# A recurrent attention with an expert layer on one core: a tabled instruction order, column sums in parts, contiguous w_out rows, u spread on chip, and the DMA crossbar from chunk 10

## The chip, the core and the metric

The kernel runs on one core of a Trainium2 chip. The metric is the device time of one execution in microseconds; before the change it is 200.19 us (median of three runs, 199.79 to 200.97). The profile of one such execution has a span of 198.7 us from the first to the last instruction, and the clock granted to TensorE was 1.000 of full speed throughout.

The engines are PE (TensorE matmul), PEld (its weight loads), DVE (VectorE), ACT (ScalarE), POOL (GpSimd) and SP (SyncE, which here only issues DMA). An engine runs its instructions in the order in which the program emits them, so the emission order is a design choice of its own.

## What is computed

An attention with a decaying state, per batch and head, whose result feeds a two-layer expert with a squared ReLU (cut from the reference):

```python
batch, n_heads, seq, head_dim = (4, 8, 768, 48)
n_tokens, d_model, d_ff = (3072, 384, 2048)

for t in range(S):                                    # per batch and head
    cur = u * k[t] (outer) v[t]
    y[t] = r[t] @ (state + cur)
    state = w[t][:, None] * state + k[t] (outer) v[t]

h = x @ w_in            # x: y, 3072 x 384;  w_in 384 x 2048
r = maximum(h, 0)
g = s * (r * r) + b
out = g @ w_out         # w_out 2048 x 384
```

Since g = s r^2 + b, the kernel computes out = s (r^2 @ w_out) + b (column sums of w_out).

## The kernel before

The sequence is cut into 6 chunks of 128 tokens; with 4 batches there are 24 chunks n, with chunk index n // 4 and batch n % 4. Two chunks make one tile T of 256 tokens for the expert layer, so there are 12 tiles. A chunk passes through these steps (cut; each is one function of the kernel):

```python
def load(n, which):     # w, r, k, v of the chunk, 192 KB each, rows of 48 floats
    nc.sync.dma_start(out=dst, in_=src[bb, :, t0 : t0 + L, :].transpose([1, 0, 2]))
def ln(n):              # ACT: log of w
    nc.scalar.activation(out=lw[:, :, 0:D], in_=cb[n]["w"], func=AF.Ln)
def cum(n):             # PE: two triangular matmuls (running sums), and column sums
    ...
def expo(n):            # ACT: E = exp of them; lam, the decay over the chunk
    ...
def mult(n):            # DVE: prd = (r, k) * E, bf16
    ...
def trans(n):           # PE: eight transposes of prd into PSUM, n < 16
    ...
def tevac(n):           # ACT: copies them to RK in SBUF
    nc.scalar.copy(out=RK, in_=c["trps"])
def dtrans(n):          # n >= 16: the same through the DMA crossbar
    nc.sync.dma_start_transpose(out=RK, in_=c["prd"]...)
def mt(n):              # PE: eight products K R^T per chunk
    ...
def mask(n):            # DVE: times the triangular mask
    ...
def ymm(n):             # PE: y = R state (4 matmuls, not for the first chunk of a batch) + M v (8)
    ...
def dmm(n): ...         # PE: k^T v (4 matmuls); supd on DVE, sscale on POOL: the new state
def yevac(n): ...       # DVE: x = y + the diagonal part (rkp, rku, yd on POOL, cd on DVE)
def xtr(n): ...         # PE: three transposes of x, evicted by ACT (n < 16); dxtr: crossbar
```

The expert layer. A "piece" is a quarter of w_in or w_out, 768 KB in fp32, loaded into a staging buffer and cast to bf16 by ACT or POOL (w_in) or DVE (w_out):

```python
def load_wout(i):
    nc.sync.dma_start(
        out=st,
        in_=moe_w_out[i * FPP * 128 : (i + 1) * FPP * 128, :].rearrange(
            "(ft p) n -> p ft n", p=128
        ),
    )

def g1(T, i):            # one group: 2 slices of 128 rows of h, 6 matmuls 128x256
    for f in range(FPQ):
        ft = i * FPQ + f
        for kt in range(KT):
            nc.tensor.matmul(
                ps[:, f, :],
                lhsT=w_in_sb[ft // FPP][:, kt, (ft % FPP) * 128 : (ft % FPP + 1) * 128],
                rhs=xT[T][:, kt, :], ...
            )
def relu(T, i): ...      # ACT: rh = max(h, 0), bf16
def square(T, i): ...    # ACT or DVE: gT = rh * rh
def g2(T, q):            # one group: 4 matmuls 128x384 of gT with w_out, 4 groups per 128 tokens
    ...
def oevac(T, tt): ...    # DVE: out = s * o + bconst
def store(T, tt): ...    # SP: 192 KB

def colsum():
    ps = psO.tile([128, d_model], FP32, name="cs_ps", tag="o")
    for ft in range(FT):
        nc.tensor.matmul(ps, lhsT=ones, rhs=w_out_sb[ft // FPP][:, ft % FPP, :], ...)
    nc.scalar.activation(out=bconst, in_=ps, func=AF.Copy, scale=b_bc)
```

All steps are entered in a plan with an assumed duration, what they depend on and the buffers they take. When the program is built, a list scheduler walks through the plan and yields the order of emission. Loads stand in one fixed chain: four chunks and u, then the four pieces of w_in, then the four of w_out, then the other chunks. Wherever the plan sees PE idle in the first 28 us, matmuls on zeros ("warm") are emitted to keep its clock up:

```python
for t, o in pl.order():
    if o["eng"] == "PE" and t < WARM:
        warm(13 if idle_from is None else int(0.8 * (t - idle_from) / 0.11))
        idle_from = t + o["occ"]
    o["fn"](*o["args"])
```

Of the kernel before, what the change touches and what calls it, by code (L numbers as in the profile page):

```python
# [18 lines left out]
U_AT = 3.5  # L19
CIE = 'APAP'  # L20
COE = 'DDDD'
VBE = 'P'
WARM = 28.0
DTK = 16
DTX = 16
# [3 lines left out]
SLACK = 0.3  # L29


class Plan:
# [9 lines left out]
    def add(self, name, eng, occ, fn, args=(), deps=(), takes=(), prio=0.0,  # L42
            lat=0.12, port=False, dma=0.0, slack=0.0):
        self.ops[name] = dict(
            name=name, eng=eng, occ=occ, fn=fn, args=args, deps=list(deps),
            takes=list(takes), prio=prio, lat=lat, port=port, dma=dma,
            slack=slack, after=None, n=len(self.ops),
        )

    def order(self):  # L50
        ops = self.ops
        end = {}
        free = {}
        port = 0.0
        dma = 0.0
        held = {tag: [] for tag in self.rings}
        queues = {}
        for o in sorted(ops.values(), key=lambda o: (o["prio"], o["n"])):
            queues.setdefault(o["eng"], []).append(o)
        out = []  # L60

        def ready(o):
            t = 0.0
            for d in o["deps"]:
                if d not in end:
                    return None
                if d == o["after"]:
                    continue
                own = ops[d]["eng"] == o["eng"] and not ops[d]["dma"]
                t = max(t, end[d] - ops[d]["lat"] if own else end[d] + o["slack"])  # L70
            for tag, _ in o["takes"]:
                h = held[tag]
                if len(h) >= self.rings[tag]:
                    for d in h[-self.rings[tag]]:
                        if d not in end:
                            return None
                        t = max(t, end[d] + o["slack"])
            return t

        while any(queues.values()):  # L80
            best = None
            for eng, q in queues.items():
                e = free.get(eng, 0.0)
                pick = None
                for o in q:
                    r = ready(o)
                    if r is None:
                        continue
                    ask = max(r, e)
                    t = max(ask, port) if o["port"] else ask  # L90
                    if pick is None or t < pick[0] - 1e-9:
                        pick = (t, ask, o)
                if pick and (best is None or pick[:2] < best[:2]):
                    best = pick
            assert best is not None, [q[0]["name"] for q in queues.values() if q]
            t, _, o = best
            queues[o["eng"]].remove(o)
            free[o["eng"]] = t + o["occ"]
            if o["port"]:
                port = t + o["occ"]  # L100
            fin = t + o["occ"] + o["lat"]
            if o["dma"]:
                dma = max(dma, t + o["occ"] + 1.0) + o["dma"]
                fin = dma + 0.9
            end[o["name"]] = fin
            for tag, last in o["takes"]:
                held[tag].append(last)
            out.append((t, o))
        self.end = end
        self.last = out  # L110
        return out
# [3 lines left out]
def kernel(  # L115
# [60 lines left out]
    u_bc = const.tile([128, HD], FP32, name="u_bc", tag="u_bc")  # L176
    s_bc = const.tile([128, 1], FP32, name="s_bc", tag="s_bc")
# [31 lines left out]
    def coords(n):  # L209
        return n // B, n % B  # L210

# [41 lines left out]
    def castv(n):  # L253
        c = cb[n]
        vb = work.tile([128, H, D], BF16, name="vb", tag="vb", bufs=6)
        cast(VBE[n % len(VBE)], vb, c["v"])
        c["vb"] = vb
# [267 lines left out]
    def load_wout(i):  # L525
        st = wst.tile([128, FPP, d_model], FP32, name="wo_st", tag="wst")
        nc.sync.dma_start(
            out=st,
            in_=moe_w_out[i * FPP * 128 : (i + 1) * FPP * 128, :].rearrange(
                "(ft p) n -> p ft n", p=128  # L530
            ),
        )
        w_out_st[i] = st
# [5 lines left out]
    def g1(T, i):  # L539
        if i == 0:  # L540
            gT[T] = mlp.tile([128, FT, TOK], BF16, name="gT", tag="gT", bufs=3)
        ps = psH.tile([128, FPQ, TOK], FP32, name="h_ps", tag="h")
        for f in range(FPQ):
            ft = i * FPQ + f
            for kt in range(KT):
                nc.tensor.matmul(  # L546
                    ps[:, f, :],
                    lhsT=w_in_sb[ft // FPP][
                        :, kt, (ft % FPP) * 128 : (ft % FPP + 1) * 128
                    ],  # L550
                    rhs=xT[T][:, kt, :],
                    start=(f == 0 and kt == 0),
                    stop=(f == FPQ - 1 and kt == KT - 1),
                )
        hs[T, i] = ps
# [9 lines left out]
    def square(T, i):  # L565
        rh = hs.pop((T, i))
        g = gT[T][:, i * FPQ : (i + 1) * FPQ, :]
        if sq_eng(T, i) == "ACT":
            nc.scalar.activation(out=g, in_=rh, func=AF.Square)  # L569
        else:  # L570
            nc.vector.tensor_tensor(out=g, in0=rh, in1=rh, op=ALU.mult)  # L571
# [38 lines left out]
    def colsum():  # L610
        ps = psO.tile([128, d_model], FP32, name="cs_ps", tag="o")
        for ft in range(FT):
            nc.tensor.matmul(
                ps,
                lhsT=ones,
                rhs=w_out_sb[ft // FPP][:, ft % FPP, :],
                start=(ft == 0),
                stop=(ft == FT - 1),
            )
        nc.scalar.activation(out=bconst, in_=ps, func=AF.Copy, scale=b_bc)  # L620
# [11 lines left out]
    def cast(letter, out, in_):  # L632
        if letter == "A":
            nc.scalar.copy(out=out, in_=in_)  # L634
        elif letter == "P":
            nc.gpsimd.tensor_copy(out=out, in_=in_)  # L636
        else:
            nc.vector.tensor_copy(out=out, in_=in_)

    def cast_in(i):  # L640
        cast(CIE[i], w_in_sb[i], w_in_st[i])

    def cast_out(i):
        cast(COE[i], w_out_sb[i], w_out_st[i])
# [7 lines left out]
    def load_u():  # L652
        nc.sync.dma_start(
            out=u_bc, in_=u.rearrange("h d -> (h d)").partition_broadcast(128)
        )

    for n in range(N):
# [9 lines left out]
        add(("rku", n), "POOL", 1.0, pool1b, (n,), [("rkp", n), "load_u"],  # L667
# [16 lines left out]
            [("prd", [("tr" if n < DTK else "tev", n)] + ([("dmm", n)] if keep else []))], P - 1, port=True)  # L684
        if n < DTK:
# [4 lines left out]
        else:  # L690
            add(("tev", n), "SP", 1.2, dtrans, (n,), [("mul", n)],
                [("RK", [("mt", n), ("ymm", n)])], P - 1000, dma=1.0, slack=0.1)
# [7 lines left out]
            [("B", [("yev", n)]), ("x", [("xtr" if n < DTX else "xev", n)])], P - 6, lat=0.2, slack=SL)  # L700
# [3 lines left out]
        if n < DTX:  # L704
# [3 lines left out]
        else:  # L708
            add(("xev", n), "SP", 0.7, dxtr, (n,), [("yev", n)] + xd, xt,
                P - 1000, dma=0.4, slack=0.1)  # L710
# [16 lines left out]
    for T in range(NT):  # L727
        P = BIG + 10 * T
        for i in range(NQ):
# [5 lines left out]
                + ([("gT", [("g2", T, 4 * CPT - 1)])] if i == 0 else []),  # L735
# [6 lines left out]
        for i in range(4 * CPT):  # L742
# [5 lines left out]
            if i:  # L748
                need.append(("g2", T, i - 1))
            take = []  # L750
            if part == 0:
                need.append("colsum")
                take = [("h" if T == NT - 1 else "o", [("oev", T, tt)])]
            add(("g2", T, i), "PE", 0.65, g2, (T, i), need, take, P + 1000 + i, lat=0.2, slack=MSL if T > 1 else 0.0)
            if part == 3:
                add(("oev", T, tt), "DVE", 0.53, oevac, (T, tt), [("g2", T, i), "colsum"],
# [3 lines left out]
    add("colsum", "PE", 2.7, colsum, (), [("co", i) for i in range(NPIECE)] + ["small2"],  # L760
        [("o", ["colsum"])], BIG, lat=0.8)
    add("small", "SP", 0.4, small, (), [], [], 12.5, dma=0.05)
    add("small2", "SP", 0.4, small2, (), [], [], 12.6, dma=0.05)
    add("load_u", "SP", 0.7, load_u, (), [], [], U_AT, dma=1.0)
    chain = []
    for n in range(N):
        for x in range(4):
# [3 lines left out]
            chain.append((10.0 * n + x, ("load", n, x)))  # L771
            add(("load", n, x), "SP", 0.6, load, (n, x), [], take,
                10.0 * n + x, dma=1.03)
    for i in range(NPIECE):
        chain.append((WIN_AT[i] + 0.01 * i, ("li", i)))
        chain.append((WOUT_AT[i] + 0.01 * i, ("lo", i)))
# [3 lines left out]
            WOUT_AT[i] + 0.01 * i, dma=2.15)  # L780
# [4 lines left out]

    for p, nm in ((13.5, "small"), (13.6, "small2"), (U_AT, "load_u")):
        chain.append((p, nm))
    chain.sort(key=lambda c: c[0])
    for a, b in zip(chain, chain[1:]):
        pl.ops[b[1]]["deps"].append(a[1])  # L790
        pl.ops[b[1]]["after"] = a[1]
# [8 lines left out]
    nc.vector.memset(ones, 1.0)  # L800
    nc.vector.memset(par, 0.0)
# [18 lines left out]
    idle_from = None  # L820
    for t, o in pl.order():
        if o["eng"] == "PE" and t < WARM:
            warm(13 if idle_from is None else int(0.8 * (t - idle_from) / 0.11))
            idle_from = t + o["occ"]
        o["fn"](*o["args"])
    if SHOW is not None:
        SHOW(pl)

# [29 lines left out]
```

The softmax here doesn't subtract the row's maximum and nothing guards it: scores larger than these inputs give would overflow.

## Time and profile before

| | before |
|---|---|
| time, median of 3 | 200.19 us |
| span of the profiled execution | 198.7 us |
| PE: g1, 576 matmuls 128x256 | 73.9 us busy |
| PE: g2, 384 matmuls 128x384 | 66.3 + 5.4 us busy |
| PE: warm matmuls | 104, 15.1 us busy |
| ACT: relu, 96 | 56.2 us, 598 ns each |
| ACT: square, 40; DVE: square, 56 | 25.2 us, 630 ns each; 29.4 us, 537 ns each |
| ACT: copy of the PE transposes, 16 | 16.1 us, 1008 ns each |
| DMA transposes: RK 8, x 8 | 3.4 and 2.3 us from issue to landing |
| chunk loads, 192 KB, 96 | 4.4 to 4.6 us from issue to landing (medians) |
| weight pieces, 768 KB, 8 | 8.3 (w_in), 7.6 (w_out) us from issue to landing |

How to read it: busy time is a sum over instructions of an engine. For PE each matmul's recorded length contains the time in which its result drains while the next one already streams, so 273 ns is not what a g1 matmul costs in a stream; the distance between the starts of neighbours is. A time from issue to landing contains the wait of the transfer behind earlier ones in the same queue.

### The profile page before, as it was taken

How to read it: one execution, taken by the hardware profiler on the slowest of the kernel's cores; microseconds unless marked ns; L12 is line 12 of the kernel's file. 1: busy time of each engine (PE TensorE's matmuls, PEld its weight loads, DVE VectorE, ACT ScalarE, POOL GpSimd, SP SyncE). 2: the span in 40 equal slices, each digit the busy share in tenths (PEclk: the TensorE clock that was granted, in tenths of full speed). 3: DMA queues.
4: the chain of work that ended last, by engine and by line, in shares of the span. 5: the costliest groups of instructions: out<-in, count | busy, mean ns of one | idle time of the engine just before them, and what ended most of it. 6: DMA issues, size and time to landing. Idle time of an engine off the chain costs nothing.

```text
span 198.7 us, 4921 instructions
## 1 busy us (share of the span) xinstructions
PE 187.0 (94%) x1928; PEld 138.9 (70%) x1928; DVE 133.1 (67%) x212; ACT 133.2 (67%) x240; POOL 114.4 (58%) x144
## 2 busy tenths in 40 slices
PE   6997888979999999999999999999999999999992
PEld 4766567745668777777776786776687778777651
DVE  6476838836977978869787686799787692222221
ACT  3446487745658999999996997690069868768000
POOL 3787932029998899959987788959981000000000
PEclk9999999999999999999999999999999999999999
DMA  6999999979999999999999899999433931111122
GB/s 125 200 175 179 299 394 371 278 145 200 188 156 197 160 195 173 200 234 195 220 169 194 186 202 190 210 236 173 128 82 75 122 98 27 43 40 40 43 79 79
DMA packets 119239, 33.29 MB, mean 168 GB/s; under 512 B 112432, under 2 KB 117680, under 8 KB 119216
## 3 DMA queue, kind: packets, MB, share of 16 engines
q1 hardware_dynamic: 119216, 32.98, 83.0%
q8 instruction: 15, 0.25, 0.6%
q14 instruction: 8, 0.07, 0.1%
HBM read 25.36 MB, written 4.72 MB: 151 GB/s over the span
## 4 chain that ended last, share of the span: by engine, by line
PE 66%; DMA 14%; SPq 11%; ACT 3%; POOL 2%; issue 2%; DVE 1%; POOLq 0%
PE o_ps L584 26%; PE h_ps L546 23%; SPq L225 9%; DMA wi_st<-in_moe_w_in_dram 5%; DMA wt<-in_w_dram 5%; DMA rkt<-in_k_dram 4%; PE mt_ps L382 3%; PE o_psh L584 3%; PE trps L340 2%; PE y_ps L419 2%; PE y_ps L410 2%; PE cums L281 1%; PE cums L284 1%; PE d_ps L435 1%; ACT rh L559 1%
## 5 line engine op out<-in xcount | busy, mean ns | idle before, releaser
L546 PE MATMUL h_ps<-xT,w_in 128*128 128x256 bf16 x576 | 73.9, 273 | 2.0 <-ACT w_in L634 1.4
L559 ACT ACTIVATE rh<-h_ps 128x512 bf16<-128x512 f32 x96 | 56.2, 598 | 23.2 <-PE h_ps L546 21.8
L584 PE MATMUL o_ps<-w_out,gT 128*128 128x384 bf16 x352 | 66.3, 326 | 0.0
L546 PEld LDWEIGHTS <-w_in 128*128 128x128 bf16 x576 | 53.7, 98 | 12.5 <-issue 1.8
L584 PEld LDWEIGHTS <-gT 128*128 128x128 bf16 x384 | 35.8, 98 | 19.2
L571 DVE TENSOR_TENSOR gT<-rh 128x512 bf16<-128x512 bf16 x56 | 29.4, 537 | 14.5 <-ACT rh L559 14.4
L237 POOL TENSOR_TENSOR rkp<-rkt 128x384 f32<-128x384 f32 x24 | 25.1, 1047 | 17.2 <-DMA rkt<-in_k_dram 17.1
L394 DVE TENSOR_TENSOR mt_sb<-mt_ps,tri_strict 128x1024 bf16<-128x1024 f32 x24 | 29.2, 1216 | 1.3 <-PE mt_ps L382 1.3
L268 POOL TENSOR_TENSOR yd<-vt,cd 128x384 bf16<-128x384 f32 x24 | 25.2, 1048 | 4.8 <-DVE cd L262 4.6
L313 DVE TENSOR_TENSOR prd<-rkt,E 128x768 bf16<-128x768 f32 x24 | 24.1, 1004 | 5.6 <-ACT E L303 4.1
L569 ACT ACTIVATE gT<-rh 128x512 bf16<-128x512 bf16 x40 | 25.2, 630 | 1.3
L248 POOL TENSOR_TENSOR rku<-rkp,u_bc 128x384 f32<-128x384 f32 x24 | 24.6, 1025 | 0.4
L303 ACT ACTIVATE E<-cums 128x768 bf16<-128x768 f32 x24 | 19.4, 806 | 7.5 <-PE cums L289 7.4
L594 DVE SCALAR_TENSOR_TENSOR o_sb<-o_ps,s_bc,bconst 128x384 f32<-128x384 f32 x22 | 13.5, 615 | 14.8 <-PE o_ps L584 13.4
L486 POOL TENSOR_TENSOR st<-stmp,l 128x384 bf16<-128x384 bf16 x16 | 18.6, 1164 | 8.3 <-DVE stmp L477 7.9
L355 ACT COPY RK<-trps 128x1024 bf16<-128x1024 bf16 x16 | 16.1, 1008 | 5.5 <-PE trps L340 5.5
L449 DVE TENSOR_TENSOR x_sb<-y_ps,yd 128x384 bf16<-128x384 f32 x24 | 13.3, 552 | 6.7 <-PE y_ps L419 5.2
L262 DVE TENSOR_REDUCE cd<-rku 128x8 f32<-128x384 f32 x24 | 13.0, 542 | 6.8 <-POOL rku L248 6.8
L232 ACT ACTIVATE logw<-wt 128x384 bf16<-128x384 f32 x24 | 12.4, 523 | 7.0 <-DMA wt<-in_w_dram 6.8
L816 PE MATMUL warm_ps<-warm_sb 128*128 128x256 bf16 x104 | 15.1, 294 | 1.1 <-DVE warm_sb L795 1.1
L636 POOL CAST vb<-vt 128x384 bf16<-128x384 f32 x24 | 13.4, 558 | 0.0
L816 PEld LDWEIGHTS <-warm_sb 128*128 128x128 bf16 x104 | 10.2, 105 | 2.7 <-DVE warm_sb L795 1.1
(52 smaller groups left out, 168.5 us busy)
## 6 DMA issues: line engine op xcount, KB each, us to landing
wt<-in_w_dram SPq DMA_DIRECT2D x24, 192.0 KB, 4.5
rkt<-in_r_dram SPq DMA_DIRECT2D x24, 192.0 KB, 4.4
rkt<-in_k_dram SPq DMA_DIRECT2D x24, 192.0 KB, 4.6
vt<-in_v_dram SPq DMA_DIRECT2D x24, 192.0 KB, 4.4
out_dram<-o_sb SPq DMA_DIRECT2D x24, 192.0 KB, 2.2
wi_st<-in_moe_w_in_dram SPq DMA_DIRECT2D x4, 768.0 KB, 8.3
wo_st<-in_moe_w_out_dram SPq DMA_DIRECT2D x4, 768.0 KB, 7.6
u_bc<-in_u_dram SPq DMA_DIRECT2D x1, 192.0 KB, 4.3
```

Of the source, the lines that this page charges most:

```text
L237: nc.gpsimd.tensor_tensor(out=rkp, in0=c["rk"][:, 0].rearrange("t h d -> t (h d)"), in1=c["rk"][:, 1].rearrange("t h d -> t (h d)"), op=AL ...
L248: nc.gpsimd.tensor_tensor(out=rku.rearrange("t h d -> t (h d)"), in0=c["rkp"], in1=u_bc, op=ALU.mult)
L268: nc.gpsimd.tensor_tensor(out=yd, in0=c["v"], in1=c["cd"].unsqueeze(2).to_broadcast([128, H, D]), op=ALU.mult,)
L303: nc.scalar.activation(out=E, in_=ps[:, :, 0:HD], func=AF.Exp)
L313: nc.vector.tensor_tensor(out=prd[:, :, :, 0:D].rearrange("t x h d -> t (x h) d"), in0=c["rk"].rearrange("t x h d -> t (x h) d"), in1=c["E ...
L394: nc.vector.tensor_tensor(out=m.rearrange("s g p t -> s (g p) t"), in0=c["mt_ps"].rearrange("s g p t -> s (g p) t"), in1=tri_strict.unsque ...
L546: nc.tensor.matmul(ps[:, f, :], lhsT=w_in_sb[ft // FPP][:, kt, (ft % FPP) * 128 : (ft % FPP + 1) * 128], rhs=xT[T][:, kt, :], start=(f == ...
L559: nc.scalar.activation(out=rh, in_=hs[T, i], func=AF.Relu)
L569: nc.scalar.activation(out=g, in_=rh, func=AF.Square)
L571: nc.vector.tensor_tensor(out=g, in0=rh, in1=rh, op=ALU.mult)
L584: nc.tensor.matmul(ps, lhsT=gT[T][:, ft, tt * 128 : (tt + 1) * 128], rhs=w_out_sb[ft // FPP][:, ft % FPP, :], start=(ft == 0), stop=(ft == ...
L816: nc.tensor.matmul(warm_ps, lhsT=warm_sb[:, 0:128], rhs=warm_sb, start=True, stop=True)
```

## The change

- The list scheduler goes. The order of emission stands as a table in the program, found beforehand by annealing. A word is a step (`g12.0` is g1 of tile 2, group 0; `vb3`, `tr0`, `li0`, `lo0`, `ci1`, `co0` the cast of v, the transposes, the loads of w_in and w_out and their casts), `+7` is seven warm matmuls, and `@A`, `@D`, `@P` override the engine of a step.
- Loads are no longer in one chain: the table mixes the weight pieces with the chunk loads.
- The column sum is cut in four parts, each after its piece of w_out; the second GEMM no longer waits for it, only the eviction of its result does. The groups of the two halves of a tile's second GEMM no longer follow one another by rule.
- A piece of w_out is loaded with four neighbouring rows to a partition (6,144 B in one run in place of four runs of 1,536 B). The rows of the hidden layer are then assigned to partitions in another way, so g1 reads its weights from w_in with a step of four columns.
- u is loaded as one row and spread over the partitions by a matmul with ones and a copy, in place of a DMA that writes it to 128 partitions.
- Transposes of r, k go through the DMA crossbar from chunk 10 on (before: 16), those of x for odd chunks from 13 and all from 18 (before: 16).
- The table assigns squares and casts to engines one by one.

The core of the diff, cut:

```diff
-VBE = 'P'
-WARM = 28.0
-DTK = 16
-DTX = 16
+VBE = 'AP'
+DTK = 10
+DTX = 18
+DK2 = 10
+DX2 = 12
+ORDER = """
+load0.0 load0.1 load_u load1.0 load0.2 ln0 load2.0 +13 cum0 load1.1 +1 u_mm exp0 load1.2 u_ev l20
+ln1 load0.3 +6 cum1 mul0 load2.1 exp1 rkp0 +7 tr0 ln2 load2.2 +1 cum2 tev0 l21 rku0 load3.0 exp2
+mul1 load3.1 +10 mt0 rkp1 cd0 +1 tr1 vb0 load1.3 msk0 tev1 +1 dmm0 rku1 load3.2 +6 mt1 mul2 li0
+rkp2 cd1 +7 tr2 load2.3 sup0 tev2 msk1 yd0 +3 ymm0 li1 ln3 rku2 yev0 +5 cum3 vb1@A load3.3 xtr0
+l22 dmm1 exp3 sup1 rkp3 xev0 +5 mt2 ymm1 mul3 li2 yd1 cd2 +5 tr3 ci0 load4.0 l23 yev1 vb2@P msk2
++6 xtr1 tev3 rku3 lo0 xev1 +7 dmm2 yd2 mt3 cd3 g10.0 sup2 ci1@A li3 msk3 ymm2 g10.1 vb3 relu0.0
+yev2 yd3 dmm3 relu0.1 sup3 g10.2 lo1 sq0.1@A sq0.0 g10.3 relu0.2 ci2@D xtr2 load4.1 ymm3 relu0.3
+xev2 yev3 g10.4 ln4 sq0.2 xtr3 sq0.3 g10.5 relu0.4 load4.2 xev3 cum4 sq0.4 relu0.5 g11.0 co0 g11.1
+relu1.0 st0 g20.0 load5.0 exp4 g11.2 relu1.1 ci3 g20.4 relu1.2 g11.3 lo2 sq0.5@A sq1.2@A colsum0
+co1 relu1.3 lo3 g11.4 sq1.0 g20.1 small2 relu1.4 g10.6 sq1.1@A mul4 load5.1 g20.5 relu0.6 rkp4 tr4
+...  (48 more lines)
+g111.6 relu11.5 g210.5 sq11.3 sq11.4@A g111.7
+relu11.6 g210.6 relu11.7 g210.3 sq11.7 g210.7 sq11.5 oev10.0 g211.0 sq11.6 oev10.1 g211.4
+store10.1 g211.1 store10.0 g211.5 g211.2 g211.6 g211.3 g211.7 oev11.0 store11.0 oev11.1 store11.1
+"""
...
+    def xbar_rk(n):
+        return n >= DTK or (n >= DK2 and n % 2 == 1)
+
+    def xbar_x(n):
+        return n >= DTX or (n >= DX2 and n % 2 == 1)
...
-                "(ft p) n -> p ft n", p=128
+                "(p ft) n -> p ft n", ft=FPP
...
-                    lhsT=w_in_sb[ft // FPP][
-                        :, kt, (ft % FPP) * 128 : (ft % FPP + 1) * 128
-                    ],
+                    lhsT=w_in_sb[ft // FPP][:, kt, :].rearrange(
+                        "p (m j) -> p j m", j=FPP
+                    )[:, ft % FPP, :],
...
-    def colsum():
-        ps = psO.tile([128, d_model], FP32, name="cs_ps", tag="o")
-        for ft in range(FT):
+    def colsum(i):
+        if i == 0:
+            os_["cs"] = psB.tile([128, d_model], FP32, name="cs_ps", tag="B")
+        for ft in range(i * FPP, (i + 1) * FPP):
...
+    def csevac():
+        nc.scalar.activation(out=bconst, in_=os_["cs"], func=AF.Copy, scale=b_bc)
...
-            out=u_bc, in_=u.rearrange("h d -> (h d)").partition_broadcast(128)
+        nc.sync.dma_start(out=u_row, in_=u.rearrange("h d -> (h d)").unsqueeze(0))
+
+    def spread_u():
+        ps = psO.tile([128, HD], FP32, name="u_ps", tag="o")
+        nc.tensor.matmul(ps, lhsT=one_row, rhs=u_row, start=True, stop=True)
+        os_["u"] = ps
+
+    def u_evac():
+        nc.vector.tensor_copy(out=u_bc, in_=os_.pop("u"))
...
-                need.append("colsum")
...
-                add(("oev", T, tt), "DVE", 0.53, oevac, (T, tt), [("g2", T, i), "colsum"],
+                add(("oev", T, tt), "DVE", 0.53, oevac, (T, tt), [("g2", T, i), "csevac", "small"],
...
-    for t, o in pl.order():
-        if o["eng"] == "PE" and t < WARM:
-            warm(13 if idle_from is None else int(0.8 * (t - idle_from) / 0.11))
-            idle_from = t + o["occ"]
-        o["fn"](*o["args"])
+    for o in pl.order(ORDER):
+        if isinstance(o, int):
+            warm(o)
+        else:
+            o["fn"](*o["args"])
```

## The prediction

> **What bounds the kernel now.** I read the busy line first, then the chain of waits, then busy time by stage, and last the timeline of the stage that the first three pointed to.
>
> ```profile
> PE 187.0 (94%) x1928; PEld 138.9 (70%) x1928; DVE 133.1 (67%) x212; ACT 133.2 (67%) x240; POOL 114.4 (58%) x144
> PE 66%; DMA 14%; SPq 11%; ACT 3%; POOL 2%; issue 2%; DVE 1%; POOLq 0%
> ```
>
> TensorE is the engine with no room, and the chain that ended last runs on it for two thirds of the span; DMA and the DMA-issuing queue hold 25% of it. The stage view says where those 25% lie (columns: length, then busy us and instruction count of PE, PEld, DVE, ACT, POOL, then clock, DMA share, GB/s).
>
> ```profile
> 0.00:25.70 25.70, 20.97 (x219) 15.20 (x219) 16.17 (x29) 11.91 (x20) 18.05 (x30) 1.00 0.97 203
> 25.70:43.70 18.00, 16.08 (x146) 12.23 (x147) 12.09 (x23) 13.21 (x22) 3.17 (x3) 1.00 0.98 300
> 43.70:59.30 15.60, 15.15 (x171) 10.04 (x170) 11.45 (x17) 9.19 (x17) 15.02 (x19) 1.00 1.11 179
> 59.30:127.00 67.70, 66.73 (x778) 52.07 (x775) 54.19 (x81) 60.97 (x119) 58.63 (x72) 1.00 1.11 194
> 127.00:161.00 34.00, 34.00 (x355) 25.23 (x353) 27.73 (x43) 20.73 (x37) 19.50 (x23) 1.00 0.74 138
> ```
>
> From 43.7 us on PE is busy all the time. Before that the 16 DMA engines are full (0.97, 0.98), and much of PE's busy time is the dummy matmuls that keep its clock up. The timeline has the stage's events (start, length, instruction, in brackets the idle time before it and what ended it).
>
> ```profile
> 24.18 1.47 ACT L634 CAST w_in<-wi_st 128x1536 bf16<-128x1536 f32 x1 [1.11 <-DMA wi_st<-in_moe_w_in_dram]
> 25.70 0.83 PE L546 MATMUL h_ps<-xT,w_in 128*128 128x256 bf16 x6 [1.39 <-ACT w_in L634]
> ...
> 33.47 0.95 DVE L638 CAST w_out<-wo_st 128x1536 bf16<-128x1536 f32 x1
> 35.44 0.96 DVE L638 CAST w_out<-wo_st 128x1536 bf16<-128x1536 f32 x1 [0.35 <-DMA wo_st<-in_moe_w_out_dram]
> 37.60 0.96 DVE L638 CAST w_out<-wo_st 128x1536 bf16<-128x1536 f32 x1 [0.17 <-DMA wo_st<-in_moe_w_out_dram]
> 39.74 0.96 DVE L638 CAST w_out<-wo_st 128x1536 bf16<-128x1536 f32 x1 [0.16 <-DMA wo_st<-in_moe_w_out_dram]
> 39.82 2.76 PE L613 MATMUL cs_ps<-w_out,ones 128*128 128x384 bf16 x16
> 43.47 1.00 POOL L237 TENSOR_TENSOR rkp<-rkt 128x384 f32<-128x384 f32 x1 [11.59 <-DMA rkt<-in_k_dram]
> 43.67 0.32 PE L281 MATMUL cums<-logw,tri_strict 128*128 128x384 bf16 x1 [1.08 <-ACT logw L232]
> ```
>
> The first GEMM waits for the first w_in piece; all eight weight pieces come in one block; the attention of chunk 4 waits behind that block; and no second GEMM may start before the whole column sum. So the end is set by PE's real work plus the time before about 43.7 us in which PE has none.
>
> The real work, by distance between starts of neighbours (a length in the timeline includes the drain):
>
> ```profile
> 50.72 0.61 PE L340 MATMUL trps<-identity,prd 128*128 128x128 bf16 x8
> 51.16 0.81 PE L584 MATMUL o_ps<-w_out,gT 128*128 128x384 bf16 x4
> 51.81 0.33 PE L410 MATMUL y_ps<-st,RK 128*128 128x96 bf16 x4
> 51.98 0.36 PE L419 MATMUL y_ps<-vb,mt_sb 128*128 128x48 bf16 x8
> 52.19 0.32 PE L281 MATMUL cums<-logw,tri_strict 128*128 128x384 bf16 x1
> ```
>
> A chunk's eight transposes take 0.44 (51.16 - 50.72), four output matmuls 0.65, the state part of y 0.17, its masked part 0.21. In the same way: cum 0.43, the M matmuls 0.33, the state update 0.17, the transpose of x 0.17, six h matmuls 0.655. Sum: 96 x 0.655 + 96 x 0.65 = 125.3 for the GEMMs; 16 x 0.163 = 2.6 for the column sum; attention 24 x (0.43 + 0.33 + 0.21) + 20 x (0.17 + 0.17) + 16 x (0.44 + 0.17) = 39.8. Together 167.7. The last matmul ends at 195.1, so 27.4 us hold no real work. Up to 43.67 PE has done four chunks without a state (4 x 1.75 = 7.0), 16 of the h groups (10.5) and the sum (2.6), 20.1 in all: 23.6 of the 27.4 lie there, and 3.8 in the 151 us after. The 3.6 us after 195.1 are the last eviction (0.62) and store.
>
> **What the Trainium skill says.** "TensorE: Matmul & The Clock Gate", section "Step-by-step: what each phase is for": weights of the next matmul load while the present one runs. The trace agrees: the masked part of y changes its 128 weight columns every 0.026 us (0.21 / 8), without a gap. Same page, "Weight-path perf modes — Fast Weight Load (FWL) and DoubleRow": the fast load takes its chunks of columns "packed or strided". "SBUF — State Buffer", section "Door 1: The DMA port swizzle", wants at least two accesses to each 16-byte line; a step of four bf16 is 8 bytes, just two to a line. No weight load of the kernel before has such a step, so no row here shows it. "DMA: Bandwidth & Descriptors", "Specifications": line rate needs at least 512 B per transfer. The trace agrees: chunk loads, whose runs are 48 floats or 192 B, come 17 in the 18.0 + 1.1 us up to 21.98, 1.125 each (175 GB/s), whereas a 768 KB weight piece takes 2.15 (39.74 - 37.60; 366 GB/s).
>
> **The change, part by part.**
>
> 1. *First GEMM earlier.* In the old issue order 16 chunk loads and the 192 KB broadcast of u precede w_in piece 0, which lands at 24.18. In the table 14 chunk loads and one 1.5 KB row of u precede it. Three slots of 1.125 fewer: landing at 20.8, cast 1.47, first h matmul at about 22.3 in place of 25.7. The table puts 4 cum, 4 transposes, 4 M, 2 y, 3 updates and 2 x ahead of it: 1.72 + 1.76 + 1.32 + 0.42 + 0.51 + 0.34 = 6.1 of work, so 16.2 without (the spreading of u counts there).
> 2. *Other work while weights arrive.* Piece 1 now lands after one chunk load more: 20.8 + 1.1 + 2.15 = 24.1, cast at 25.6; piece 2 at 27.4, cast on DVE at 28.4; w_out piece 0 after chunk 4's first load at about 30.7; the fourth w_in piece 32.9, second w_out piece 35.0; then three chunk loads (38.4) and the last two pieces (42.7). Second-GEMM groups and the column sum start with each piece instead of at 44.09. Between 22.3 and 43.7 there are 10.5 of h, up to 2.6 of sums, 5.2 of the output groups that need pieces 0 and 1, 0.9 left of chunks 0 to 3 and 2 to 3 of chunks 4 and 5: about 22 for 21.4 us. Supply and demand match so nearly that I leave 2.5 us idle, most of it between 23.6 and 25.6, where only one w_in piece is there. That makes 18.7 against 23.6: 4.9 saved.
> 3. *Crossbar from chunk 10.* Six chunks lose the PE transpose (6 x 0.44 = 2.6), and x of 13 and 15 moves off PE while 16 moves back (net 0.17): 2.8 saved on the full engine. ACT loses six evictions of 1.01; DMA takes six more transposes with 3.4 us to landing. In the table nine or more PE groups stand between such a transpose and its first reader, some 5 us, so this is hidden unless its queue is late.
> 4. *w_out rows of 6,144 B.* Four pieces, perhaps 0.2 each: 0.8 off the DMA stream, none of it clearly on the path; I count 0. In exchange the 576 weight loads of the first GEMM read w_in with a step of four. They have 0.109 us each (0.655 / 6) and packed loads were seen to need no more than 0.026, so a fourfold cost would still just fit: 0.
> 5. *Engines swapped.* The table puts 67 squares on ACT (40 before), 29 on DVE, 12 of the v casts on ACT. ACT: 133.2 + 27 x 0.63 + 12 x 0.52 - 6.0 - 0.5 = 150, DVE about 120, POOL about 106, all below 190. No gain on PE, and less room on ACT.
> 6. *Later stalls.* I keep the 3.8 us of scattered loss: an annealed order packs tighter but has less slack. The tail stays: the last two evictions now follow one another, as the last of them did.
>
> Sum: 4.9 + 2.8 = 7.7, from 200.2 to 192.5.
>
> **The rivals.**
>
> *The fixed order stalls.* Every engine executes in order, and a table made for assumed durations waits wherever the chip differs. For it: ACT was already 90% busy between 59.3 and 127 (60.97 of 67.70) and now takes more; loads stand in odd order (a load of chunk 11 before chunk 9's). Against it: the old static order too lost only 3.8 us in 151. If it holds, 4 to 8 us come back as waits of h for rh or of y for its mask: 196 to 200.
>
> *The strided weights are slow.* If a load takes over 0.109 us, each of the 576 h matmuls pays. At 0.13 us that is 576 x 0.02 = 12 us, and the time 204. For it: nothing in the trace has this step. Against: the fourfold room above. I give it one in twelve.
>
> *The early gain is given back.* Chunk data and weights share one full DMA stream; PE that starts sooner may run out sooner, between 44 and 56 us, when chunks 4 and 5 must come through. For it: the stream is full to 127 us. Against: chunk 4's k lands at about 37 instead of 43.5. Then only the 2.8 of part 3 remain: 197.
>
> *More than expected.* If the table removes the 2.5 us of part 2 and half of the scattered loss, 188.
>
> **Range and chances.** 192.5 is the sum; stalls by the first rival pull the upper end to 198, the last one sets the lower at 188. Faster by 2% means below 196.2, and the sum has 3.7 us of room: 0.76. Within 2%: 0.15, for the stalling order or the gain given back. Slower: 0.09, the strided weights or a badly stalled order.
>
> **What would show it.** Right: first h matmul at 22 to 23 us; w_out casts spread from 31 to 43; the first output group before 34; transposes on PE in 10 chunks; h groups still 0.65 apart; scattered idle of PE after 44 us at most 4 us. Wrong: w_in weight loads well above the 98 ns of before and h groups over 0.7 apart; PE waits of over 1 us for rh, RK or xT, or for DMA between 44 and 60; ACT over 95% in a stage where PE has gaps.

## The result and the profile after

The changed kernel takes 193.51 us (median of four runs, 192.63 to 193.68) against 200.3 us before: ratio 0.965, 95% interval 0.961 to 0.969. The span of the profiled execution falls from 198.7 to 191.5 us.

The busy line and the chain of waits of the kernel after:

```profile
PE 181.7 (95%) x1859; PEld 140.6 (73%) x1859; DVE 125.1 (65%) x188; ACT 143.8 (75%) x272; POOL 105.8 (55%) x131
PE 63%; SPq 17%; DMA 5%; ACT 4%; issue 4%; DVE 3%; POOL 1%; DVEq 0%
```

PE is still the engine with no room: its busy time fell by 5.3 us, and ACT took on 10.6. By stage (columns as in the same view of before; the stages end at the first h matmul, at about the end of the column sums, and so on):

```profile
0.00:23.57 23.57, 19.77 (x209) 13.75 (x209) 15.00 (x29) 13.77 (x22) 15.70 (x26) 1.00 1.09 203
23.57:43.70 20.13, 19.26 (x186) 15.67 (x183) 12.28 (x20) 17.80 (x33) 5.97 (x6) 1.00 1.01 301
43.70:60.00 16.30, 15.32 (x172) 11.55 (x171) 10.78 (x16) 11.76 (x24) 12.77 (x17) 1.00 1.08 176
60.00:100.00 40.00, 40.00 (x458) 31.95 (x457) 31.36 (x46) 35.10 (x72) 31.52 (x39) 1.00 1.19 197
```

The second stage now keeps PE busy for 96% of its length (19.26 of 20.13; before 16.08 of 18.00), and none of that is dummies: the last one starts at 22.1, before the first h matmul. The timeline of the kernel after shows how (start, length, instruction, idle time before it):

```profile
20.52 1.47 ACT L683 CAST w_in<-wi_st 128x1536 bf16<-128x1536 f32 x1 [1.48 <-DMA wi_st<-in_moe_w_in_dram]
21.90 1.00 ACT L400 COPY RK<-trps 128x1024 bf16<-128x1024 bf16 x1
22.80 0.48 ACT L557 COPY xT<-xt_ps 128x384 bf16<-128x384 bf16 x1
23.57 0.84 PE L591 MATMUL h_ps<-xT,w_in 128*128 128x256 bf16 x6
...
30.68 0.96 DVE L687 CAST w_out<-wo_st 128x1536 bf16<-128x1536 f32 x1 [0.47 <-DMA wo_st<-in_moe_w_out_dram]
31.70 0.81 PE L629 MATMUL o_ps<-w_out,gT 128*128 128x384 bf16 x4
34.31 0.81 PE L659 MATMUL cs_ps<-w_out,ones 128*128 128x384 bf16 x4
34.68 0.96 DVE L687 CAST w_out<-wo_st 128x1536 bf16<-128x1536 f32 x1 [3.03 <-DMA wo_st<-in_moe_w_out_dram]
39.59 0.96 DVE L687 CAST w_out<-wo_st 128x1536 bf16<-128x1536 f32 x1 [2.35 <-DMA wo_st<-in_moe_w_out_dram]
41.51 0.96 DVE L687 CAST w_out<-wo_st 128x1536 bf16<-128x1536 f32 x1 [0.63 <-DMA wo_st<-in_moe_w_out_dram]
42.88 0.81 PE L659 MATMUL cs_ps<-w_out,ones 128*128 128x384 bf16 x4
```

The pieces of w_out come spread out, and the first output group starts at 31.70 in place of 44.09, a microsecond after its piece has landed (its cast starts at 30.68).

**Where the 7.2 us are.** I count the matmuls of every kind up to a point and give each the stream cost of the prediction (0.655 us for a group of h, and so on). What is left is time in which PE did no real work.

| without real work, us | before | after | saved |
|---|---|---|---|
| up to the first h matmul (25.7; 23.57) | 20.0 | 17.4 | 2.6 |
| from there to about 43.6 | 3.4 | 1.8 | 1.6 |
| later, to the last matmul (195.1; 187.9) | 4.4 | 4.2 | 0.2 |
| real work itself | 167.3 | 164.5 | 2.8 |
| sum to the last matmul | 195.1 | 187.9 | 7.2 |

After the last matmul both kernels have the same 3.6 us of eviction and store. The border between the first two rows is only the moment at which h starts. What has to be explained is their sum, 4.2 us, and the 2.8 us of real work.

### The profile page after: what moved, and what is told of

The parts are those of the page before. It is cut to its first block, busy times and chain, and to the rows that moved or that the text cites. A ratio compares the mean times of both kernels' runs of the same rounds, so it can differ in the third digit from the quotient of the medians.

```text
span 191.5 us, 4784 instructions
## 1 busy us (share of the span) xinstructions
PE 181.7 (95%) x1859; PEld 140.6 (73%) x1859; DVE 125.1 (65%) x188; ACT 143.8 (75%) x272; POOL 105.8 (55%) x131
## 4 chain that ended last, share of the span: by engine, by line
PE 63%; SPq 17%; DMA 5%; ACT 4%; issue 4%; DVE 3%; POOL 1%; DVEq 0%
PE h_ps L591 24%; PE o_ps L629 24%; SPq L270 14%; DMA wi_st<-in_moe_w_in_dram 4%; PE mt_ps L427 3%; PE o_psh L629 3%; PE y_ps L464 2%; DMA vt<-in_v_dram 2%; PE d_ps L480 2%; PE y_ps L455 2%; DVE gT L616 1%; PE cums L326 1%; PE cums L329 1%; SPq L696 1%; PE trps L385 1%
## 5 line engine op out<-in xcount | busy, mean ns | idle before, releaser
L591 PE MATMUL h_ps<-xT,w_in 128*128 128x256 bf16 x576 | 77.8, 273 | 0.9 <-DVE w_in L687 0.6
L629 PE MATMUL o_ps<-w_out,gT 128*128 128x384 bf16 x352 | 69.7, 326 | 0.6 <-DVE o_sb L639 0.6
L591 PEld LDWEIGHTS <-w_in 128*128 128x128 bf16 x576 | 61.0, 114 | 7.6 <-DVE w_in L687 0.7
L614 ACT ACTIVATE gT<-rh 128x512 bf16<-128x512 bf16 x67 | 40.2, 629 | 0.5
L282 POOL TENSOR_TENSOR rkp<-rkt 128x384 f32<-128x384 f32 x24 | 30.3, 1262 | 17.7 <-DMA rkt<-in_k_dram 17.7
L616 DVE TENSOR_TENSOR gT<-rh 128x512 bf16<-128x512 bf16 x29 | 16.8, 594 | 1.9 <-ACT rh L604 1.6
L531 POOL TENSOR_TENSOR st<-stmp,l 128x384 bf16<-128x384 bf16 x16 | 14.7, 917 | 2.3 <-DVE stmp L522 2.3
L685 POOL CAST vb<-vt 128x384 bf16<-128x384 f32 x12 | 6.8, 563 | 11.9 <-DMA vt<-in_v_dram 11.9
L400 ACT COPY RK<-trps 128x1024 bf16<-128x1024 bf16 x10 | 10.2, 1016 | 2.7 <-PE trps L385 2.3
L372 POOL TENSOR_TENSOR l<-lam,par 128x8 f32<-128x8 f32 x20 | 6.9, 348 | 8.3 <-ACT lam L352 8.3
```

Of the source, the lines that this page charges most:

```text
L282: nc.gpsimd.tensor_tensor(out=rkp, in0=c["rk"][:, 0].rearrange("t h d -> t (h d)"), in1=c["rk"][:, 1].rearrange("t h d -> t (h d)"), op=AL ...
L591: nc.tensor.matmul(ps[:, f, :], lhsT=w_in_sb[ft // FPP][:, kt, :].rearrange("p (m j) -> p j m", j=FPP)[:, ft % FPP, :], rhs=xT[T][:, kt, : ...
L629: nc.tensor.matmul(ps, lhsT=gT[T][:, ft, tt * 128 : (tt + 1) * 128], rhs=w_out_sb[ft // FPP][:, ft % FPP, :], start=(ft == 0), stop=(ft == ...
```

## The experiments

The theory reads this table as causes: 2.8 us of PE work moved to the crossbar, 2.6 us from an earlier first GEMM, 1.6 us from work that fits between the weights' arrivals. The main rival is that the order itself brings the gain. In the first four runs the parts were added to the kernel before, under its old list scheduler; in the others they were taken out of the tabled kernel, or the theory's explanation was put to the test. "Tabled kernel" is the kernel after; differences to it are differences of the two ratios times 200.3 us, and uncertain by 0.9 to 1.5 us. Each ratio is to the kernel before as it ran beside that variant, with medians of 200.57 to 200.95 us.

**Crossbar alone under the list scheduler (b_xbar).**

```diff
-DTK = 16
-DTX = 16
+DTK = 10
+DTX = 18
+DX2 = 12
...  (and the plan's durations for the crossbar steps as in the change)
```

> The kernel before with only the crossbar from chunk 10 (x: odd chunks from 13, all from 18), list scheduler kept. Theory (7.2 us = 2.9 crossbar + 2.2 first GEMM earlier + 1.9 second GEMM with the pieces + 0.2): PE loses 2.8 us of real work and the time falls by 2.5 to 3.0, ratio 0.986. Rival (the tabled order brings the gain, the crossbar is hidden or costs): ratio 0.995 or more, with new PE waits for RK after 85 us.

Measured: 220.15 us, ratio 1.098 (1.093 to 1.102), some 19 us slower. The theory as stated fell, and the rival was far too mild. The timeline of this kernel, first DVE's products prd of chunks 10 to 14, then the DMA-issuing queue:

```profile
75.89 0.96 DVE L320 TENSOR_TENSOR prd<-rkt,E 128x768 bf16<-128x768 f32 x1
82.44 0.95 DVE L320 TENSOR_TENSOR prd<-rkt,E 128x768 bf16<-128x768 f32 x1
83.92 1.15 DVE L320 TENSOR_TENSOR prd<-rkt,E 128x768 bf16<-128x768 f32 x1 [0.52 <-ACT E L310]
91.42 0.94 DVE L320 TENSOR_TENSOR prd<-rkt,E 128x768 bf16<-128x768 f32 x1
102.98 1.38 DVE L320 TENSOR_TENSOR prd<-rkt,E 128x768 bf16<-128x768 f32 x1 [1.20 <-DMA RK<-prd]
```

```profile
97.61 0.95 SPq L232 DMA_DIRECT2D wt<-in_w_dram  x1
98.67 1.97 SPq L369 DMA_TRANSPOSE RK<-prd  x1
```

Chunk 10's product is ready at 76.85, and its transpose is issued at 98.67. In those 21.8 us the queue, which runs in order, issues 19 chunk loads and 4 stores. With the four prd buffers full, DVE then waits for the transpose (last line of the first block), and the attention stands still while PE eats up the GEMM work it has; from 100 to 120 us PE has 13.1 us without real work, where the kernel before has 1.2. A late issue need not cost: in the kernel before, chunk 16's transpose is issued 14.1 us after its product, and from 120 to 140 us PE has 0.2 us without work. The clock line of the page shows the next cost:

```profile
PEclk9999999999999999999655799559999999999999
```

Each digit is the clock in tenths over a slice of 5.5 us. PE waits for DVE's products 1.8 us up to 104.4, 2.6 us up to 111.6 and 2.2 us up to 135.3, and is granted only half to 0.7 of its clock in the slices from 104 to 126 and from 136 to 147 us; the record of one group of h, 0.83 us long at full clock, is 1.44 us long there.

**Layout alone (b_layout).**

```diff
-                "(ft p) n -> p ft n", p=128
+                "(p ft) n -> p ft n", ft=FPP
-                    lhsT=w_in_sb[ft // FPP][:, kt, (ft % FPP) * 128 : (ft % FPP + 1) * 128],
+                    lhsT=w_in_sb[ft // FPP][:, kt, :].rearrange("p (m j) -> p j m", j=FPP)[:, ft % FPP, :],
```

> The kernel before with only the w_out rows contiguous and, with it, w_in read by a step of four. Theory: nothing on the path, ratio 0.997 to 1.003; weight loads of w_in some 114 ns in place of 98, h groups still 0.655 us apart; w_out pieces perhaps 0.2 us apart less. Rival (strided weights cost PE time): h groups over 0.67 apart, ratio above 1.007.

Measured: 200.53 us, ratio 1.002 (0.996 to 1.008). The strided loads themselves do take longer, which the source view of this kernel shows (minimum, median, maximum in ns); packed they took 95/98/99:

```profile
L546 PEld LDWEIGHTS <-w_in x576: 111/113/135, 25.7 to 180.7; 128*128 128x128 bf16 x192
L546 PE MATMUL h_ps<-xT,w_in x576: 269/273/302, 25.7 to 180.8; 128*128 128x256 bf16 x192
```

The 15 ns lie beside the matmul before: in the tabled kernel two groups of h still take 1.31 us of stream. The rival fell. The longer w_out rows do speed up their transfer, to 6.7 us from issue to landing in place of 7.6 (medians), and the last piece lands 1.2 us earlier (38.49 in place of 39.72). Nothing comes of it here: DVE starts its cast at 39.54 in place of 39.74, and PE, with h groups up to 39.87, starts the column sum no sooner. In the tabled kernel the early stage goes with the DMA stream (a_ubc below), so the shorter transfers may be worth something there; the tabled kernel with the old rows was not run, and up to about 1.2 us of its early gain may be theirs.

**Early stage alone under the list scheduler (b_early).**

```diff
+LOADS = """
+0.0 0.1 u 1.0 0.2 2.0 1.1 1.2 0.3 2.1 2.2 3.0 3.1 1.3 3.2 li0 2.3 li1 3.3 li2 4.0 lo0
+li3 lo1 4.1 4.2 5.0 lo2 lo3 small2 small
+"""
...  (u spread on chip and column sum in four parts as in the change, the sums at priority 50)
```

> The kernel before with the order of transfers of the table up to the last w_out piece, u spread on chip and the column sum in four parts, all placed by the old list scheduler; crossbar and layout as before. Theory: first h matmul near 23.5 us, output groups from 32 us, time down by 3 to 4.5, ratio 0.978 to 0.985. Rival (the annealed order of the compute steps is needed for that): less than 1.5 us, ratio above 0.992.

Measured: 200.1 us, ratio 0.997 (0.992 to 1.001). The first h matmul came at 24.29, but by 43.7 PE had 23.1 us without work, as before. Pieces arrived in time and were cast late: w_in piece 2, landed at 26.66, on ACT at 30.14, the last two w_out pieces, landed at 39.97 and 42.21, on DVE at 45 to 48 us.

**All parts under the list scheduler (b_all)**, the three edits above together; the engines of squares and casts stay as before.

> All parts of the change under the old list scheduler, without the table. Theory: the parts add, 6 to 7 us less, ratio 0.965 to 0.970, as the tabled kernel within 1 us. Rival (the table itself is worth much): ratio above 0.975, and PE has gaps after 44 us that the tabled kernel hasn't.

Measured: 217.95 us, ratio 1.087 (1.083 to 1.092). The parts do not add without the order; the crossbar's loss rules. Chunk 10's transpose is issued 21.5 us after its product, and from 100 to 140 us PE has 21.4 us without work; up to 43.5 us, though, it has 21.5, 1.9 less than before.

**PE transposes back into the table (a_petr).**

```diff
-DTK = 10
+DTK = 16
-DK2 = 10
+DK2 = 16
...  (tr10 to tr15 put just ahead of tev10 to tev15; sup10 and yev13 moved forward)
```

> The tabled kernel with the transposes of r, k of chunks 10 to 15 back on PE and ACT (each put just ahead of its eviction in the table; two DVE steps moved forward for a legal order). Theory (crossbar = real PE work removed): PE gets 6 x 0.44 = 2.6 us back, so 2.3 to 3.3 us more than the tabled kernel, ratio to before 0.977 to 0.983. Rival (the crossbar pays for nothing, the order does): within 1 us of the tabled kernel, ratio 0.970 or less.

Measured: 197.36 us, ratio 0.983 (0.980 to 0.985), 3.5 us more than the tabled kernel. By the count, PE has 2.6 us more real work and 1.1 us more without; between 80 and 100 us the latter is 1.5 more. So the crossbar as such is worth its PE work and a little more, given the table.

**Column sum in one block, output groups behind it (a_onesum).** In the table colsum0 to colsum2 and g20.0, g20.4, g20.1, g20.5, g20.6 are moved, the sums just ahead of colsum3, the groups just behind it.

> The tabled kernel with the four column-sum parts in one block behind the last w_out piece and the five output groups that stood before it moved behind it, as in the rule of before. Theory: PE had no idle time between 30 and 43.7 us, so the 3.25 us of output groups and 1.95 us of sums taken out of there leave 3.5 to 5.2 us idle, ratio to before 0.983 to 0.991. Rival (other work slips in or the early stage is bound elsewhere): less than 1.5 us more.

Measured: 195.84 us, ratio 0.975 (0.973 to 0.978), 2.0 us more. The direction is the theory's, the size between it and the rival: 3.7 us more without work by 43.5 us, of which PE makes up 1.5 later (after 43.5 us 2.6 us without work in place of 4.2). Most of that comes at once, from 43.5 to 60 us, with 0.3 us without work in place of 1.4: the block of ready groups fills waits that the tabled kernel had there.

**Loads ahead of the transposes (a_late).** In the table 34 load words of later chunks are moved ahead of tev10 to tev15, six each (four for tev15).

> The tabled kernel with six later chunk loads (four for chunk 15) put ahead of each crossbar transpose of r, k of chunks 10 to 15 in the DMA-issuing queue, nothing else moved. Theory (the crossbar pays only while its transposes aren't queued behind loads, which cost the queue 0.7 to 1.0 us each): transposes issue 4 to 6 us later, PE waits for RK through the M matmuls, 5 to 15 us more than the tabled kernel. Rival (some other property of the list schedule made the crossbar variant slow): within 2 us.

Measured: 211.56 us, ratio 1.054 (1.048 to 1.061), 18 us more: more than the theory's range, in its direction. The delays add up from chunk to chunk, which the theory had left out: the transposes of chunks 10 to 13 are issued 9.3, 15.4, 20.4 and 23.2 us after their products (3.0 to 4.1 in the tabled kernel). In this kernel, the view of waits and the timeline of PE:

```profile
PE mt_ps L426 <- DMA RK<-prd: 13.7, 4, 4.9
```

```profile
93.28 0.61 PE L426 MATMUL mt_ps<-RK 48*128 48x128 bf16 x8 [4.89 <-DMA RK<-prd]
101.12 0.51 PE L426 MATMUL mt_ps<-RK 48*128 48x128 bf16 x8 [3.27 <-DMA RK<-prd]
109.08 0.40 PE L426 MATMUL mt_ps<-RK 48*128 48x128 bf16 x8 [2.48 <-DMA RK<-prd]
```

PE waits for the transposes themselves, 13.7 us in all; the rest is a lower clock after such waits (0.967 on the mean) and work that runs late. Moving nothing but loads in the DMA queue was enough: it isn't the transposes that are slow. The same queue in the tabled kernel, for comparison, where chunk 10's product (first line) is ready at 80.26:

```profile
79.26 1.00 DVE L358 TENSOR_TENSOR prd<-rkt,E 128x768 bf16<-128x768 f32 x1
82.44 0.70 SPq L270 DMA_DIRECT2D rkt<-in_k_dram  x1
83.25 1.87 SPq L407 DMA_TRANSPOSE RK<-prd  x1
85.17 0.57 SPq L653 DMA_DIRECT2D out_dram<-o_sb  x1
85.85 1.30 SPq L407 DMA_TRANSPOSE RK<-prd  x1
```

**Fewer loads ahead (b_xbar_ring4).**

```diff
-    ain = ctx.enter_context(tc.tile_pool(name="ain", bufs=8))
+    ain = ctx.enter_context(tc.tile_pool(name="ain", bufs=4))
-        dict(w=8, rk=8, v=8, ...
+        dict(w=4, rk=4, v=4, ...
```

(against b_xbar)

> The crossbar variant under the list scheduler with four load buffers in place of eight, in the pool and in the plan, so that loads can't run far ahead. Theory (transposes stuck behind prefetches): most of the 19 us vanish, ratio 0.985 to 1.01 in place of 1.098. Rival (the crossbar itself is too slow for the list schedule): 1.06 or more.

Measured: 201.1 us, ratio 1.003 (0.997 to 1.009). 19 of the 19 us are gone, as the theory said: the first transpose is issued at 82.62, 5.0 us after its product. (With four buffers the scheduler can also find another order of the steps, so this run alone does not tell the loads from the order; a_late does.) But nothing is gained on the kernel before. The profiled execution, at 203.0 us the slowest of four, has some 7 us without work between 120 and 160 us, of which PE is idle in the record for 4.3 (2.9 of them in two waits for crossbar transposes of x); the rest includes a clock of 0.91 from 140 to 160 us. At the median, 201.1 us beside 200.57 for the kernel before, some 3.3 us of losses outweigh the 2.8 us of PE work; where they lie in such an execution no trace shows.

**u by DMA again (a_ubc).** load_u writes u to 128 partitions as before; the matmul and the copy are left out.

> The tabled kernel with u written to all partitions by a DMA as before, the spreading matmul and its copy left out, order unchanged. Theory (the DMA stream sets the early stage): every transfer after the third comes one slot of 1.0 to 1.1 us later, PE, which has no idle time from 30 to 43.7 us, ends 0.7 to 1.2 us later, ratio to before 0.969 to 0.972. Rival (the first h matmul is set by ACT and PE order, not by DMA): within 0.3 us of the tabled kernel.

Measured: 195.3 us, ratio 0.974 (0.969 to 0.980), 1.8 us more. The first w_in cast starts at 22.24 in place of 20.52, the first h matmul at 25.29 in place of 23.57: both exactly 1.72 later, so the early stage goes with the DMA stream. The chunk load behind u lands at 7.66 in place of 5.94, and what follows comes 1.7 us later too: in this place the broadcast takes 1.7 us of the stream. In the kernel before it lands 1.08 us after the load ahead of it, the 1.1 of a chunk load that I had booked; why it takes longer here is open. The rival fell.

**Engines as before (a_engold).** All `@` of squares, v casts and w_in casts taken out of the table, VBE = 'P'.

> The tabled kernel with the engines of before for squares (40 on ACT, 56 on DVE), v casts (POOL) and w_in casts (ACT, POOL in turn), order unchanged. Theory of the prediction (no gain on PE from the swap): within 1.5 us of the tabled kernel, ratio 0.965 to 0.973. Rival (the order lives by its engines): 2 to 6 us more, with PE waits for rh or w_in.

Measured: 195.31 us, ratio 0.973 (0.968 to 0.978), 1.6 us more. Between the two: PE waits 2.0 us in three for v casts on POOL (tabled kernel: 1.6 in two for those on ACT), 1.4 for an eviction on DVE (0.6) and 1.0 for a w_in cast on ACT (0.6 for one on DVE). The swap is worth something between nothing and 3 us in this order; the two theories are not told apart.

**Cast engines and priorities under the list scheduler (b_early2).**

```diff
-CIE = 'APAP'
+CIE = 'AADP'
-WARM = 28.0
+WARM = 20.0
...  (priority of the w_out casts 45 -> 20)
```

(against b_early)

> The early-stage variant of the list scheduler with w_in pieces 0, 1 cast on ACT, 2 on DVE, 3 on POOL, the w_out casts raised in priority on DVE, and no dummy matmuls planned after 20 us. Theory (the early stage lost its gain to casts that came late, 0.8 us for w_in and 1.5 us for w_out): 1.5 to 3 us less than before, ratio 0.985 to 0.992. Rival (the order of PE and ACT steps as such): ratio 0.994 or more.

Measured: 200.93 us, ratio 1.002 (0.996 to 1.008). The time says rival, the trace says more. By the count the early stage did win: 21.1 us without work by 60 us, against 24.4 in the kernel before and 20.6 in the tabled one. Over 1 us of the 21.1 is this variant's own: with no dummies planned after 20 us, the clock is 0.78 on the mean from 20 to 26 us, and the first two groups of h are 1.44 and 1.48 us long in place of 0.83. Then it is given back: 4.1 us without work between 80 and 100 alone, as the stage view of this kernel shows:

```profile
80.00:84.00 4.00, 3.05 (x49) 1.90 (x48) 3.67 (x7) 3.57 (x9) 3.49 (x6) 1.00 0.92 169
84.00:88.00 4.00, 3.28 (x41) 2.73 (x40) 2.50 (x4) 2.81 (x7) 3.05 (x5) 1.00 1.08 277
```

In these 20 us PE starts 9 groups of h and 5 of output, against 10 and 12 in the tabled kernel. It waits 2.4 us in four waits for steps of ACT and DVE, and ACT in turn three times, 2.3 us in all, for the w of a next chunk, once here (timeline of the same kernel). That the late data cause PE's waits is likely, but not shown:

```profile
85.72 0.52 ACT L238 ACTIVATE logw<-wt 128x384 bf16<-128x384 f32 x1 [1.19 <-DMA wt<-in_w_dram]
```

**First h earlier still (a_swap).**

```diff
-... xtr1 tev3 rku3 lo0 xev1 +7 dmm2 yd2 mt3 cd3 g10.0 sup2 ci1@A ... relu0.0
+... xtr1 xev1 tev3 rku3 lo0 +7 g10.0 dmm2 yd2 mt3 cd3 sup2 relu0.0 ci1@A ...
```

> The tabled kernel with three words moved: the copy of chunk 1's x ahead of the copy of chunk 3's transposes on ACT, the first h group ahead of chunk 2's state update and chunk 3's M on PE, the first relu ahead of the second w_in cast. Theory (first h waits for ACT, 1.5 us after its weights are cast): first h at 22.5 in place of 23.57, 0.3 to 0.8 us less than the tabled kernel, ratio 0.961 to 0.964. Rival (the weights' arrival sets the stage whatever PE starts with): no difference, within 0.3 us.

Measured: 193.55 us, ratio 0.964 (0.959 to 0.969), no difference to the tabled kernel. The first h matmul did come at 22.16, 1.4 us earlier, and by 43.5 us nothing was left of it (19.8 us without work; tabled 19.2). Until the third w_in piece is cast (DVE, 27.26 in the tabled kernel) PE only has what two pieces allow, and starting it sooner only makes it wait longer. The rival held. No variant beat the tabled kernel.

## Why the prediction was right, and where it was not

Predicted were 192.5 us, measured 193.51; predicted 7.7 saved, measured 6.8 by the medians and 7.2 by the spans. By its steps:

1. *First GEMM earlier: the weights' arrival right, the step behind it not.* The weights were to land at 20.8 (the cast starts at 20.52) and h was to start at 22.3 (23.57). The step assumed that h follows its cast at once. In fact ACT did two more copies first, of chunk 3's transposes and of chunk 1's x (21.90 and 22.80 in the timeline above), and h needs the latter. PE had 17.4 us without work up to there in place of 16.2. The run with the copies swapped shows that this 1.2 us was not on the path, and so that the start of h as such is worth nothing: what counts is when the weights come. Of the three slots of transfers saved, that of u is shown to matter by itself: put back into the table, it costs 1.8 us.
2. *Work while weights arrive: right, a little better than stated.* 2.5 us idle were allowed, 1.8 measured. Together with the first step 19.2 against the predicted 18.7, and 4.2 saved where 4.9 was predicted: this is the term that was mis-sized, by 0.7 us. Taking the early output groups out costs 2.0 us, which shows that they fill time that would else be lost. How much of the 4.2 is owed to the faster transfer of the w_out rows is open.
3. *Crossbar: 2.8 us of PE work, exactly as counted.* "Hidden unless its queue is late" was the right condition, but it carried far more than the sentence let see: without an order that keeps loads back, the same edit costs 19 us (b_xbar), and with 34 loads moved it costs 18 (a_late). The prediction looked at the distance between a transpose and its reader on PE; what mattered as much was the distance between the product and the issue of its transpose in the DMA queue: 3.0 us in the tabled kernel, 21.8 under the list scheduler.
4. *Layout: 0 under the list scheduler; in the table not measured alone.* The loads grew from 98 to 113 ns (medians) and stayed hidden. The rival let each matmul pay once a load takes over 109 ns; at 113 the groups of h still stand 0.655 us apart, so the recorded length of a load, like that of a matmul, is not what it costs in a stream. The w_out pieces got faster by 1.2 us in all, more than the 0.8 allowed.
5. *Engines: "no gain on PE" is not confirmed.* Undoing the swap costs 1.6 us, uncertain by 1.3. As a term of the sum it had been left at 0. Taken out one at a time, crossbar, early groups, u and engines cost 3.5, 2.0, 1.8 and 1.6 us, 8.9 in all and more than the 6.8 gained: they aren't shares of one sum. The table with none of them was not run, so what the annealed order is worth without them stays open.
6. *Later stalls: kept.* 4.4 before, 4.2 after; the annealed order neither stalled nor packed tighter.

Of the prediction's own signs, the w_out casts (30.68 to 41.51), the first output group (31.70) and the distance of h groups (0.655) came as stated; the first h matmul (23.57, for 22 to 23) and the time without work after 44 us (4.2, for at most 4) just missed. Of the rivals, the stalling order did not come (ACT at 35.10 of 40 us between 60 and 100 never held PE up by more than 0.3 us at an h group). The strided weights did not cost. The early gain given back did not happen here, but it is what happened to the list scheduler with the same early stage (b_early2). So the sum was right to 0.9 us, the two mechanisms behind it are the ones that the runs show, and what it left unsaid is that its two main terms belong to the order: both the crossbar and the early stage, put in alone, gave no gain. Not tried was an order that differs from the table's in other ways but paces the loads as it does; whether pacing alone lets the list scheduler keep both gains stays open, with four load buffers as the nearest answer: it undid the loss, not more.

## What to carry to other kernels

When work moves from a full engine to a queue that runs in order, look at what stands ahead of it in that queue, and hold prefetches back that nobody needs yet: the same transposes are worth 3.5 us or cost 19, by the loads before them. Count the real work of the bound engine up to a few points in time and compare; the time without work says which stage a change can touch, and whether a gain made early survives. And test a part both ways, added to the old kernel and taken from the new one: here the first says loss, the second says gain, and both are true of their order.

## What was not expected of the hardware

- "DMA: Bandwidth & Descriptors", section "Issuing engines are not separate DMA queues", of the Trainium skill calls the time to initiate a DMA usually small relative to the DMA itself. In these traces the issuing queue is a resource of its own, with 17% of the chain of waits in the tabled kernel: a chunk load holds it some 0.4 to 1.9 us in the tabled kernel after 70 us, and a crossbar transpose of 128x1024 bf16 1.25 to 3.0 us (median 1.73) for 4.0 us from issue to landing.
- Writing one row of 1,536 B to 128 partitions delays what follows by 1.7 us when it is put into the tabled kernel, more than the 1.1 us between the landings of chunk loads of the same 192 KB in runs of 192 B. In the kernel before it lands 1.08 us after the load ahead of it.
- Weight loads with a step of four bf16 take 113 ns in place of 98 (medians). They grew by a sixth and stayed hidden beside matmuls of 256 columns, whose starts stay 109 ns apart.
- Pieces of w_out, 768 KB each, land 1.93 us apart in runs of 6,144 B (b_layout) and 2.14 us apart in runs of 1,536 B (kernel before), on the mean of the three distances.
